# Cosine attention and a two-layer product on one core: quad 4 transposed in a visit of the first output stage, two quads' loads asked within the W1 stage, other amounts between the visits

## The chip, the cores and the metric

The kernel runs as one program on one core of a Trainium2 chip. The metric is device microseconds of one execution. The engines are named as in the profile: PE is TensorE (matmuls, transposes), PEld its weight loads, ACT is ScalarE, DVE is VectorE, POOL is GpSimd, SP is SyncE, which here only asks for DMAs. POOL asks for DMAs too, on a queue of its own.

## The reference

Inputs: q, k, v of shape (8, 12, 448, 64) in float32, tau = 0.1, w_in (768, 2048) and w_out (2048, 768). The core of it:

```python
q_n = q / (np.linalg.norm(q, axis=-1, keepdims=True) + 1e-06)
k_n = k / (np.linalg.norm(k, axis=-1, keepdims=True) + 1e-06)
scores = np.matmul(q_n, k_n.transpose(0, 1, 3, 2)) / tau
attn = softmax(scores)                      # max taken off, +1e-9 in the divisor
x = (attn @ v).transpose(0, 2, 1, 3).reshape(3584, 768)
h = x @ w_in
out = (h * np.cos(h)) @ w_out               # (3584, 768) float32
```

`softmax` stands here for the three lines of the reference that compute it.

## The kernel before

**Tiling.** Four heads of one batch entry make a quad: 8 entries x 12 heads are 24 quads, numbered 0 to 23, three to a batch entry. A quad's scores are computed in 7 blocks (j = 0 to 6) of 64 keys for all 448 queries and four heads; written (quad, block), as (3,6). A block is 4 matmuls of 64x64 (`scores`, L592) into two PSUM banks, and one Exp on ACT of 128x896 out of them into a tile E (L608). The kernel takes no maximum off, since normalised vectors bound the scores. When a quad's 7 blocks are done, `gather` (L629) multiplies the E tiles with V (28 matmuls, L637), DVE copies the result to AVs (L644), `sums` (L711) sums E over the keys and makes reciprocals, and `product` (L748, on POOL) multiplies both into xT, the input of the W1 product. R holds the reciprocals, read back from DRAM by SP's DMAs. For quad 5 the spreading is done by PE and DVE (`spread_out`).

**Before a quad's scores** come: the loads of its Q and K (`load_qk`, L442, two DMAs of 448 KB on SP's queue, into one of three buffers Qf and Kf), the squares on POOL (L491), their sums on DVE (L495), a Ln, an Exp, an add and a reciprocal for the norm (`inverse`, L521 to L530), the scaling on POOL (`scale`, L542, tiles Qn and Kn), and the transposition to qT and kT. For quads up to 5 the transposition is done by PE (`transpose`, L557): 7 matmuls of L564 for Qn, 7 for Kn, each into one PSUM bank, and two copies out of PSUM, on DVE (L575) or on ACT (L572). Later quads are transposed by DMA (`turn`, L580), asked for by SP.

**Stages.** Quads 0 to 2 are done ahead (to about 32 us). Then a loop over the batch entries c = 0 to 7 (L1093) runs two stages for each entry. The *W1 stage* computes h in 8 pairs of 128 columns (`m1_part`, L774, 12 matmuls a pair) and for each pair h*cos(h) by four operations: ACT rounds (L792), DVE reduces the argument (L793), ACT takes the Sin (L795), DVE multiplies (L798) into gT; the last pair is cut in halves. The *output stage* multiplies gT with w_out (`m2`, L833, 6 x 16 matmuls for c = 0) and, between these matmuls, does the scores of later quads. Exp and Sin need different tables on ACT; L412 loads one, 1.3 us, at each change of stage.

**Visits.** The scores of an output stage come in visits (`visits_of`, `visit`): three blocks each, after the second block of a visit the gather that is owed from the quad ended before. The first output stage (c = 0) does quads 3 to 7 in 12 visits: visit 1 is (3,0), (3,1), (3,2); visit 2 is (3,3), (3,4), (3,5); visit 3 is (3,6), (4,0), (4,1); visit 4 is (4,2), (4,3), gather of quad 3, (4,4), and the transposes of quad 5; visit 5 is (4,5), (4,6), (5,0); visit 6 (5,1), (5,2), gather of quad 4, (5,3), and so on. Ahead of visit 1 and after each visit, `fill(n)` (L1141) puts n matmuls of L833; for c = 0 the amounts are the 13 entries of `FILLS` (L860). Every block, gather and PE transposition in a visit takes the next of three slots of two PSUM banks (`slot`, L892) in turn, so the fourth after a given one must wait until that one has been read out.

**Orders.** PE does its work in the order in which the program writes it down. The order of the other engines is made by the planner (`pass_`, L121): a simulated time and for each operation a due time, worked back from PE's order. Operations are numbered as they are written down. `LEADS` (L107) adds a shift to the due times of a run of numbers: (first number, how many, shift in us), a negative one for earlier. Before the change (578, 8, -2.3) names the norm and the scaling of quad 10 and the first block (8,0) with its Exp, at the start of the second output stage; (1169, 8, -11.0) names operations of pairs 4 and 5 of a later W1 stage; (811, 8, -0.5) the table load, norm and scaling at the start of the third output stage. The orders hold through semaphores: an engine that comes to an operation whose data isn't there waits, and everything behind it on that engine with it. DMAs asked for by SP keep the order of the text for quads from 5 on, and those asked for by POOL all do.

**The places of the change.** In the W1 stage of c = 0, after pair 4, PE transposes quad 3 into the two banks of `last`; after pair 5, quad 4 into those of `av`; Q is copied out by DVE, K by ACT (L1122 to L1124). Pairs 6 and 7 then use the same banks. The loads of quads 6 and 7 stand behind the norms of quads 3 and 4 (L1087 to L1090): they may start as soon as the buffer, in which quads 3 and 4 lie, has been scaled. Quad 6 is squared early, into the tiles R (`SPARE`, L470, L1127), and its square sums are taken in visit 1 of c = 0 (L1177); quad 7 is squared in visit 3 (L906).

Of the kernel before, what the change touches and what calls it, by code (L numbers as in the profile page):

```python
# [20 lines left out]
class Planner:  # L21
# [10 lines left out]
    FIRST, LAST, CROWD = 0.6, 1.0, 1.11  # L32
# [49 lines left out]
    def flow(self, until):  # L82
# [22 lines left out]
                return o  # L105

    LEADS = (  # L107
        (1169, 8, -11.0),
        (578, 8, -2.3),
        (811, 8, -0.5),  # L110
    )

# [192 lines left out]
def bass_cosine_attention__then__act_gcu_kernel(  # L305
# [19 lines left out]
    FIRST = 3  # L325
# [51 lines left out]
    P = Planner()  # L377
# [64 lines left out]
    def load_qk(qd, after=()):  # L442
        return [load_one(qd, w, after=after) for w in range(2)]
# [413 lines left out]
                    op("sp", 0.6, lambda e, sg=sg, dst=dst: e.dma_start(dst, osb[so].ap()[64 * sg:64 * sg + 64, :]),  # L857
                       r=[("o", so, 0), ("o", so, 1)], w=[("out", t, sg)], dma=("store", so, sg), moves=0.56)

    FILLS = {0: [17, 12, 12, 6, 3, 6, 0, 13, 0, 14, 6, 3, 0]}  # L860
    STEPS = [35,28,21,21,21,21, 0, 0]
    MOST, WE = 14, (3, 2)
    ROUNDS = [[FIRST, FIRST + 1], [FIRST + 2]] + [[i, i + 1] for i in range(FIRST + 3, NQ, 2)]
# [32 lines left out]
    def visit(what):  # L896
        for qd, j in what:
            if j == 0:
                begin(qd)
            if j is None:  # L900
                gather(qd, slot())
            else:
                scores(NJ * qd + j, slot())
        for qd, j in what:
            if j == 0 and FIRST < qd < NQ - 3:
                norm_a(qd + 3, [o for o in P.ops if o.eng == "dve"][-1:])  # L906
            if j == 3 and FIRST < qd < NQ - 4:
                load_qk(qd + 4)
            if (qd, j) == (FIRST + 1, 3):
                bs = slot()  # L910
                for w in range(2):
                    transpose(FIRST + 2, w, bs + w)
            if j == NJ - 1 and qd + 2 < NQ:
                if qd > FIRST:
                    turn(qd + 2)
# [169 lines left out]
    P.arrange(HEAD)  # L1085
    ended = [o for o in P.ops if o.eng == "act"]
    norm_b(FIRST, after=ended[-1:])  # L1087
    load_qk(FIRST + 3)
    norm_b(FIRST + 1, after=ended[-1:])
    load_qk(FIRST + 4)  # L1090

    done = NJ * FIRST
    for c in range(B):  # L1093
# [20 lines left out]
        for pr in range(NNB // 2):  # L1114
            m1_part(c, pr, at_bank[pr], order if pr < early else (0, 1), late if pr < early else 0, NKC)
            if pr == 0 and c >= EC:
                if c == EC:
                    carried.extend(r for r in ROUNDS if r[-1] == done // NJ - 1)
                while carried:
                    sums(carried.pop(0), av if c > EC else last)  # L1120
            m1(c, pr, at_bank[pr])
            if c == 0 and 4 <= pr <= 5:  # L1122
                for w in range(2):
                    transpose(FIRST + pr - 4, w, (last, av)[pr - 4] + w, eng=("dve", "act")[w])  # L1124
        if c == 0:
            norm_a(FIRST + 2, [o for o in P.ops if o.eng == "dve"][-1:])
            adds = [square(SPARE, w, "pool") for w in range(2)]  # L1127
# [103 lines left out]
```

## Time and profile before

| what | us |
|---|---|
| median of 3 runs | 419.74 (418.62 to 419.95) |
| the profiled execution, its own time | 419.27 |
| its span in the trace | 417.5 |
| PE busy | 408.4 |
| ACT busy | 305.1 |
| DVE busy | 266.0 |
| POOL busy | 209.3 |

The span is what the trace covers, from the first to the last instruction of the execution; 1.8 us of the execution's time lie around it. "Busy" counts an engine's instructions from start to end; a matmul's end is modelled and overlaps the next one's start. In a timeline row stand start, duration, engine, line of the kernel, operation, tiles written and read, shape and count; in brackets the idle time ahead of it and what ended it. Rows of equal operations that follow one another are merged.

### The profile page before, as it was taken

How to read it: one execution, taken by the hardware profiler on the slowest of the kernel's cores; microseconds unless marked ns; L12 is line 12 of the kernel's file. 1: busy time of each engine (PE TensorE's matmuls, PEld its weight loads, DVE VectorE, ACT ScalarE, POOL GpSimd, SP SyncE). 2: the span in 40 equal slices, each digit the busy share in tenths (PEclk: the TensorE clock that was granted, in tenths of full speed). 3: DMA queues.
4: the chain of work that ended last, by engine and by line, in shares of the span. 5: the costliest groups of instructions: out<-in, count | busy, mean ns of one | idle time of the engine just before them, and what ended most of it. 6: DMA issues, size and time to landing. Idle time of an engine off the chain costs nothing.

```text
span 417.5 us, 8622 instructions
## 1 busy us (share of the span) xinstructions
PE 408.4 (98%) x3629; PEld 216.7 (52%) x3629; DVE 266.0 (64%) x359; ACT 305.1 (73%) x422; POOL 209.3 (50%) x145
## 2 busy tenths in 40 slices
PE   7999998999999999999999999999999999999997
PEld 7454544445554545555555555554554555555565
DVE  5887986638857549654985429845872328736931
ACT  6999899978888768897787747987797657605700
POOL 3668948996289862588419762477403113000000
PEclk9999999999999999999999999999999999999999
DMA  8999997999349994199617993099303523021023
GB/s 270 260 252 216 270 198 150 209 294 262 90 89 238 248 269 107 42 224 249 154 16 179 167 338 98 10 220 174 91 2 82 129 67 101 1 77 38 2 69 82
DMA packets 67223, 62.97 MB, mean 151 GB/s; under 512 B 36384, under 2 KB 59632, under 8 KB 67184
## 3 DMA queue, kind: packets, MB, share of 16 engines
q1 hardware_dynamic: 54816, 50.57, 47.9%
q0 software_dynamic: 12288, 11.80, 17.8%
q8 instruction: 28, 0.46, 0.4%
q14 instruction: 11, 0.09, 0.1%
q10 hardware_dynamic: 80, 0.05, 0.0%
HBM read 54.79 MB, written 11.15 MB: 158 GB/s over the span
## 4 chain that ended last, share of the span: by engine, by line
PE 80%; ACT 7%; DVE 5%; POOL 3%; DMA 2%; issue 1%; SPq 1%; POOLq 0%
PE PS L833 32%; PE PS L774 31%; PE PS L601 7%; PE PS L637 6%; ACT E L608 4%; PE PS L724 3%; DVE gT L798 2%; DVE ar L793 1%; DMA Qf<-in_q_dram 1%; DMA Kf<-in_k_dram 1%; POOL Qn L542 1%; POOL sqq L491 1%; PE PS L810 1%; ACT ar L676 1%; DVE AVs L644 1%
## 5 line engine op out<-in xcount | busy, mean ns | idle before, releaser
L608 ACT ACTIVATE E<-PS 128x896 bf16<-128x896 f32 x168 | 143.5, 921 | 20.5 <-PE PS L601 19.2
L833 PE MATMUL PS<-W,gT 128*128 128x384 bf16 x880 | 153.4, 327 | 0.0
L774 PE MATMUL PS<-xT,W 128*128 128x448 bf16 x768 | 147.7, 353 | 0.4 <-POOL xT L748 0.3
L833 PEld LDWEIGHTS PS<-W,gT 128*128 128x128 bf16 x880 | 81.9, 98 | 69.1 <-issue 16.0
L774 PEld LDWEIGHTS PS<-xT,W 128*128 128x128 bf16 x768 | 74.3, 98 | 71.3 <-issue 1.5
L792 ACT ACTIVATE ar<-PS 128x896 int32<-128x896 f32 (+1 forms) x72 | 58.8, 827 | 47.0 <-PE PS L774 46.9
L793 DVE SCALAR_TENSOR_TENSOR ar<-ar,PS 128x896 f32<-128x896 int32 (+1 forms) x72 | 69.2, 980 | 34.0 <-ACT ar L792 34.0
L748 POOL TENSOR_TENSOR xT<-AVs,R 128x896 bf16<-128x896 f32 x20 | 41.7, 2089 | 65.9 <-DMA R<-rscr 65.9
L798 DVE TENSOR_TENSOR gT<-PS,ar 128x896 bf16<-128x896 f32 (+1 forms) x72 | 69.3, 983 | 1.9 <-ACT ar L795 1.6
L795 ACT ACTIVATE ar<-ar 128x896 f32<-128x896 f32 (+1 forms) x72 | 60.6, 861 | 8.5 <-DVE ar L793 7.8
L851 DVE COPY osb<-PS 128x384 f32<-128x384 f32 x54 | 30.0, 556 | 53.6 <-PE PS L833 52.9
L542 POOL TENSOR_TENSOR Qn<-Qf,rr 128x896 bf16<-128x896 f32 x21 | 35.4, 1685 | 44.5 <-DVE rr L530 44.4
L601 PE MATMUL PS<-qT,kT 64*64 64x448 bf16 x672 | 48.9, 358 | 2.8 <-DVE kT L575 1.4
L644 DVE COPY AVs<-PS 128x896 f32<-128x896 f32 x21 | 22.8, 1088 | 35.3 <-PE PS L637 35.3
L491 POOL TENSOR_TENSOR sqq<-Qf 128x896 bf16<-128x896 f32 x21 | 35.2, 1677 | 7.3 <-DVE n L495 5.5
L491 POOL TENSOR_TENSOR sqk<-Kf 128x896 bf16<-128x896 f32 x21 | 35.2, 1676 | 6.2 <-DVE Kn L542 6.1
L542 POOL TENSOR_TENSOR Kn<-Kf,rr 128x896 bf16<-128x896 f32 (+1 forms) x22 | 36.7, 1666 | 0.0
L637 PE MATMUL PS<-E,Vb 64*64 64x448 bf16 x588 | 31.5, 350 | 0.4 <-ACT E L608 0.4
L601 PEld LDWEIGHTS PS<-qT,kT 64*64 64x64 bf16 x672 | 15.2, 105 | 27.3 <-issue 10.9
L451 POOL DMA_DIRECT2D Vb<-in_v_dram x24 | 18.1, 755 | 16.7 <-PE PS L601 10.3
L495 DVE TENSOR_REDUCE n<-sqk 128x14 f32<-128x896 bf16 (+2 forms) x24 | 24.9, 1039 | 1.8 <-POOL sqk L491 1.2
L495 DVE TENSOR_REDUCE n<-sqq 128x14 f32<-128x896 bf16 (+2 forms) x24 | 24.8, 1037 | 0.8 <-POOL sqq L491 0.6
(68 smaller groups left out, 200.5 us busy)
## 6 DMA issues: line engine op xcount, KB each, us to landing
Qf<-in_q_dram SPq DMA_DIRECT2D x24, 448.0 KB, 5.1
out_dram<-osb SPq DMA_DIRECT2D x54, 192.0 KB, 2.8
Kf<-in_k_dram SPq DMA_DIRECT2D x23, 448.0 KB, 6.1
R<-rscr SPq DMA_DIRECT2D x40, 224.0 KB, 4.4
Vb<-in_v_dram POOLq DMA_DIRECT2D x24, 224.0 KB, 5.9
W<-in_moe_w_in_dram POOLq DMA_DIRECT2D x4, 768.0 KB, 10.7
W<-in_moe_w_out_dram POOLq DMA_DIRECT2D x4, 768.0 KB, 12.5
Kf<-in_k_dram SPq DMA_DIRECT2D x1, 320.0 KB, 4.6
```

The lines of the kernel that those rows point to most:

```text
L491: op(eng, (1.64 if eng == "pool" else 1.05) * n, lambda e: e.tensor_tensor(dst, src, src, ALU.mult), r=cut(nm + "f", s, part), w=at, after ...
L495: return op("dve", 0.05 + 0.94 * n, lambda e: e.tensor_reduce(out=n2[u].ap()[:, H * w:H * w + H] if part == ALL[0] else jr(n2[u], w, part) ...
L542: lambda e: e.tensor_tensor(n[u].ap()[:, j0:j1].rearrange("p j r d -> p r j d"), f[s].ap()[:, :, j0:j1], rb, ALU.mult),
L601: ins = e.matmul(bank(bs + r, S, 64 * a, 64 * a + 64), kT[u].ap()[64 * r:64 * r + 64, j, a, :], qT[u].ap()[64 * r:64 * r + 64, :, a, :], s ...
L608: act("exp", 0.806, lambda e: e.activation(E[es].ap(), two(bs), ACT.Exp, bias=0.0, scale=INV_TAU), r=pair(bs), w=[("E", es)], chain="E")
L637: ins = e.matmul(bank(bs + a, S, 64 * r, 64 * r + 64), Vb[vs].ap()[64 * a:64 * a + 64, r, j, :], E[es[j]].ap()[64 * a:64 * a + 64, r, :], ...
L774: ins = e.matmul(bank(bk + i2), W1.ap()[:, i, 128 * nb:128 * nb + 128], xT[c % 2].ap()[:, i, :], start=(i == 0), stop=(i == NKC - 1))
L792: op("act", 0.055 + 0.375 * n, lambda e: e.activation(ai, src, ACT.Identity, bias=0.25, scale=INV2PI), r=bs, w=at)
L793: op("dve", 0.06 + 0.47 * n, lambda e: e.scalar_tensor_tensor(a, ai, -2.0 * math.pi, src, ALU.mult, ALU.add), r=bs + at, w=at)
L795: act("sin", 0.09 + 0.375 * n, lambda e: e.activation(a, a, ACT.Sin, bias=GUARD * math.pi / 2.0, scale=GUARD), r=at, w=at)
L798: op("dve", 0.07 + 0.47 * n, lambda e: e.tensor_tensor(gT.ap()[:, f0:f1, col:col + S], src, a, ALU.mult), r=bs + at, w=[("g", c % 2, f) fo ...
L833: ins = e.matmul(bank(bk, HW), gT.ap()[:, f, col:col + 128], W2.ap()[:, f, HW * h:HW * h + HW], start=(f == 0), stop=(f == NNB - 1))
```

## The change

Five edits. (1) Quad 4 is no longer transposed after pair 5 of the first W1 stage but at the end of visit 2 of the first output stage (after (3,5)), in a slot of its own, so that the visits behind it take their slots one place further on; both its copies are on DVE. (2) Quad 3 is transposed where it was, and its K copy moves from ACT to DVE. (3) The loads of quads 6 and 7 are written down after pairs 4 and 5 of the W1 stage, each behind the last operation of its pair (the DVE operation of L798). (4) `FILLS` of c = 0 has other entries; their sum stays 92. (5) Two of the three `LEADS` are others. Nothing that is computed changes.

```diff
     LEADS = (
-        (1169, 8, -11.0),
-        (578, 8, -2.3),
+        (585, 1, 3.1),
+        (560, 4, -19.9),
         (811, 8, -0.5),
     )
...
-    FILLS = {0: [17, 12, 12, 6, 3, 6, 0, 13, 0, 14, 6, 3, 0]}
+    FILLS = {0: [18, 12, 0, 9, 3, 10, 0, 15, 0, 16, 6, 3, 0]}
...
                 load_qk(qd + 4)
+            if (qd, j) == (FIRST, 5):
+                bs = slot()
+                for w in range(2):
+                    transpose(FIRST + 1, w, bs + w, eng=("dve", "dve")[w])
             if (qd, j) == (FIRST + 1, 3):
...
     norm_b(FIRST, after=ended[-1:])
-    load_qk(FIRST + 3)
     norm_b(FIRST + 1, after=ended[-1:])
-    load_qk(FIRST + 4)
...
             m1(c, pr, at_bank[pr])
-            if c == 0 and 4 <= pr <= 5:
+            if c == 0 and pr in (4,5):
+                load_qk(FIRST + 3 + (4,5).index(pr), after=P.ops[-1:])
+            if c == 0 and pr == 4:
                 for w in range(2):
-                    transpose(FIRST + pr - 4, w, (last, av)[pr - 4] + w, eng=("dve", "act")[w])
+                    transpose(FIRST, w, last + w, eng=("dve","dve")[w])
```

`FIRST` is 3.

## The prediction

> **What bounds the kernel now.** First the head of the page: span and busy time of each engine.
>
> ```profile
> span 417.5 us, 8622 instructions
> ...
> PE 408.4 (98%) x3629; PEld 216.7 (52%) x3629; DVE 266.0 (64%) x359; ACT 305.1 (73%) x422; POOL 209.3 (50%) x145
> ```
>
> TensorE (PE) is busy for all but 9.1 of 417.5 us. The change takes no matmul out and adds none, so it can only win or lose PE's waits. The next view is the busy time of each engine in stretches of the span, read for where PE does not fill its stretch.
>
> ```profile
> 44.00:52.00 8.00, 7.92 (x56) 4.47 (x54) 7.04 (x9) 6.67 (x9) 7.98 (x8) 1.00 1.20 267
> 52.00:57.00 5.00, 4.61 (x36) 2.36 (x35) 4.96 (x8) 4.68 (x7) 0.74 (x2) 1.00 1.30 203
> ...
> 62.00:67.00 5.00, 4.52 (x66) 2.36 (x64) 1.43 (x3) 4.68 (x8) 4.06 (x3) 1.00 0.55 124
> 67.00:72.00 5.00, 4.38 (x67) 1.96 (x70) 3.99 (x7) 4.54 (x7) 4.80 (x3) 1.00 0.96 156
> ...
> 82.00:90.50 8.50, 8.50 (x85) 3.67 (x83) 4.05 (x7) 7.41 (x11) 8.50 (x5) 1.00 1.08 271
> 90.50:111.00 20.50, 20.50 (x131) 10.39 (x129) 16.31 (x17) 16.11 (x21) 12.05 (x9) 1.00 0.96 231
> ...
> 148.00:417.50 269.50, 266.35 (x2149) 141.57 (x2148) 160.64 (x202) 179.60 (x235) 100.24 (x63) 1.00 0.48 114
> ```
>
> Columns: stretch, its length, then PE, weight loads, VectorE (DVE), ScalarE (ACT), GpSimd (POOL), clock, DMA share, GB/s. The clock is 1.00 throughout. The change lies between 44 and 90.5. There PE lacks 0.08 + 0.39 + 0.48 + 0.62 = 1.57 us. After 148 it lacks 3.15 us, and the chain of waits says where:
>
> ```profile
> 414.39 0.36 DVE osb L816
> ```
>
> The last PE work is over at 414.4, so 3.1 of the 3.15 us is the closing store; no wait is left there to win. Each wait of the first output stage stands in PE's timeline (start, duration, line, tiles, count, idle before and its releaser):
>
> ```profile
> 46.69 0.55 PE L564 MATMUL PS<-ident,Qn 128*128 128x128 bf16 x7
> ...
> 47.47 4.70 PE L774 MATMUL PS<-xT,W 128*128 128x448 bf16 x24
> 52.01 2.93 PE L833 MATMUL PS<-W,gT 128*128 128x384 bf16 x17
> 54.86 0.57 PE L601 MATMUL PS<-qT,kT 64*64 64x448 bf16 x8
> 55.83 0.38 PE L601 MATMUL PS<-qT,kT 64*64 64x448 bf16 x4 [0.39 <-DVE gT L798]
> ...
> 58.20 0.76 PE L601 MATMUL PS<-qT,kT 64*64 64x448 bf16 x12
> ...
> 62.72 0.82 PE L601 MATMUL PS<-qT,kT 64*64 64x448 bf16 x8
> 63.97 1.52 PE L637 MATMUL PS<-E,Vb 64*64 64x448 bf16 x28 [0.43 <-ACT E L608]
> ```
>
> ```profile
> 66.98 0.57 PE L601 MATMUL PS<-qT,kT 64*64 64x448 bf16 x8
> 68.17 0.38 PE L601 MATMUL PS<-qT,kT 64*64 64x448 bf16 x4 [0.61 <-DVE kT L575]
> ```
>
> The rows hold: the transposes of quad 4, the last W1 matmuls, the first 17 of L833, the scores of visit 1 (two blocks, then the third), of visit 2 and visit 4, the gather of quad 3, and visit 5. A matmul of L833 takes (54.86 - 52.01)/17 = 0.168 us from start to start, a block of scores 0.19 (0.76 for three, less the pipelined end), the two transposes 47.47 - 46.69 = 0.78. The printed idle understates a wait, because a row counts a matmul's pipelined end as busy. From start to start, the third block of visit 1 loses 55.83 - (54.86 + 0.38) = 0.6 us, the gather 0.7 with the block before it (63.97 against 62.72 + 0.38 + 0.19 of slower block starts), the third block of visit 5 0.8 (68.17 against 66.98 + 0.38).
>
> **Part 1: quad 4 leaves the W1 stage.** What happens at its end is set by DVE, with ACT beside it:
>
> ```profile
> 44.26 0.62 DVE L575 COPY qT<-PS 128x896 bf16<-128x896 bf16 x1
> ...
> 49.48 2.09 DVE L798 TENSOR_TENSOR gT<-PS,ar 128x896 bf16<-128x896 f32 x2 [0.56 <-ACT ar L795]
> ...
> 53.62 2.15 DVE L798 TENSOR_TENSOR gT<-PS,ar 128x896 bf16<-128x896 f32 x3
> 55.81 1.08 DVE L495 TENSOR_REDUCE n<-sqq 128x14 f32<-128x896 bf16 x1
> ```
>
> ```profile
> 45.03 0.91 ACT L572 ACTIVATE kT<-PS 128x896 bf16<-128x896 bf16 x1
> 46.89 0.92 ACT L792 ACTIVATE ar<-PS 128x896 int32<-128x896 f32 x1 [0.94 <-PE PS L774]
> ...
> 54.54 1.28 ACT L412 ACT_TABLE_LOAD   x1
> ...
> 61.38 4.16 ACT L608 ACTIVATE E<-PS 128x896 bf16<-128x896 f32 x5
> ```
>
> The row at 55.81 is the first reduction that DVE does when the stage is over. PE gives up 0.78 us of transposes. The first L833 matmul would come at 52.01 - 0.78 = 51.2. ACT gives up both copies at L572, 0.9 us each; DVE gives up one copy (qT of quad 4) and takes one (kT of quad 3), so its work stays: from 44.26 on two copies of 0.54, seven wide operations of 1.00 (the second of the pair at 49.48) and four halves of 0.55, together 10.3 us. It now ends at 53.62 + 2.15 = 55.8, so it idles 1.2 us on the way: it queues for the transposes that leave, and for a Sin behind the ACT copy. Of this I leave it 0.45 (it has finished what is ready at about 47.3, and ACT's row for the next pair, at 46.89, ends at 47.8). DVE ends at 55.0, 0.8 sooner (bounds 0 and 1.2). The table load of 1.28 and the first Exp follow the last Sin and come 0.8 sooner too, near 55.1. PE arrives at visit 1 after 18 matmuls: 51.2 + 18 x 0.168 = 54.25, and its third block waits for 55.05: 0.4 instead of 0.6. **Gain 0.2.**
>
> The Trainium skill (VectorE: DVE Perf Modes, Specifications) places ScalarE nearer PSUM and VectorE nearer SBUF, which speaks against giving a copy out of PSUM to DVE. The rows have 0.62 us on DVE (44.26) against 0.91 on ACT (45.03), so the measurement decides for DVE; were the page's placement to rule the time and the copy to cost DVE 0.91 as well, DVE would end 0.3 us later and the gain of 0.2 be gone.
>
> **Part 2: quad 4 in visit 2.** Visit 2 follows the third block of visit 1 by 58.20 - 55.83 = 2.37 us (12 matmuls as before), so it starts at 57.4. How soon Exp follows its scores: the scores of visit 3 in the chain of waits, whose Exp is the row at 61.38 above.
>
> ```profile
> 61.02 0.34 PE PS L601 x4
> ```
>
> Exp starts 0.36 after its scores, steps by (4.16 - 0.92)/4 = 0.81 and frees its banks 0.95 after its start. The transposes take the slot of block (3,3), whose Exp runs 57.8 to 58.7; PE is there at 57.4 + 0.57 = 58.0 and **waits 0.7**. They run to 59.5, and no matmuls of L833 follow (the third entry of the amounts is 0). Block (3,6) goes at once. Block (4,0) needs the slot of (3,5), free at 57.8 + 1.62 + 0.95 = 60.4, and the two DVE copies, 59.2 + 1.1 = 60.3. PE is there at 59.7: **0.7 more**. Queued behind it are (4,1) and all of PE's later work. Added: 1.4 us. ACT alone sets 1.3 of it, so that is the lower bound; if a reduction of 1.08 us (row 55.81) runs ahead of the copies it is 2.5.
>
> **Part 3: what the new amounts take off.** ACT runs ahead: Exp of (3,6) starts near 60.25 instead of 61.38. PE is behind by 11 matmuls (30 done, not 41), which it owes later as cover. After visit 3 come 9 instead of 6: PE reaches the gather of quad 3 at 60.95 + 0.1 + 1.5 + 0.4 = 62.95, and its last Exp is done at 60.25 + 1.62 + 0.95 = 62.8, so of that wait 0.6 goes. The gather ends 1 us sooner, hence the DVE copy behind it and the two copies of quad 5 (66.5 instead of 68.1), while PE reaches the block that needs them at 66.5: the wait of 0.8 becomes 0 to 0.6; I take half off, 0.4. Then there are short waits of the weight loads:
>
> ```profile
> PEld PS L601 <- ACT E L608: 1.0, 4, 0.3
> ```
>
> With ACT a microsecond ahead and 10, 15 and 16 matmuls in place of 6, 13 and 14 I take off 0.6 of the 1.0 (bounds 0 and 1.0).
>
> **Part 4: the loads of quads 6 and 7.** Four DMAs of 448 KB, on SP's queue:
>
> ```profile
> 37.23 0.37 SPq L439 DMA_DIRECT2D Qf<-in_q_dram  x1
> ...
> 42.16 0.37 SPq L439 DMA_DIRECT2D Kf<-in_k_dram  x1
> 63.68 0.37 SPq L439 DMA_DIRECT2D Qf<-in_q_dram  x1
> ```
>
> SP now asks for them from 37.23 to 42.16 and then for nothing before 63.68. Behind gT of pairs 4 and 5 (49.48 to 51.57 now, some 0.7 sooner after) they are asked at about 49.9 to 51.2. No other request stands behind them in that time, so the new wait holds nothing else on SP. Landing takes, for the first Q and the last K:
>
> ```profile
> DMA to landing us min/median/max: 7.0/7.0/7.0
> ```
>
> ```profile
> DMA to landing us min/median/max: 9.1/9.1/9.1
> ```
>
> That is 44.2 to 51.3, one in 2.35 us. Asked late, they land at about 57, 59, 61.5 and 64. GpSimd needs them:
>
> ```profile
> 47.08 1.69 POOL L491 TENSOR_TENSOR R<-Qf 128x896 bf16<-128x896 f32 x1
> ...
> 56.98 1.67 POOL L491 TENSOR_TENSOR sqq<-Qf 128x896 bf16<-128x896 f32 x1 [4.26 <-DVE n L495]
> ...
> 61.97 1.69 POOL L542 TENSOR_TENSOR Qn<-Qf,rr 128x896 bf16<-128x896 f32 x1 [1.67 <-DVE rr L530]
> ...
> 85.02 4.15 POOL L748 TENSOR_TENSOR xT<-AVs,R 128x896 bf16<-128x896 f32 x2
> ```
>
> The squares of quad 6 (47.08 and right behind it) must wait. They fall into the idle 4.26 us ahead of 56.98 and after it: about 57 to 58.7 and 59.2 to 60.9. Qn of quad 5 starts at 61.97 now and can start then. So those two are covered. The two squares of quad 7 (56.98 now) are pushed behind Kn of quad 5, near 64.3, into a stretch where GpSimd is nearly full (8.50 of 8.50 us in 82 to 90.5). Of 3.4 us pushed back, 1.0 returns by the earlier Qn and 1.1 in the idle time of 62 to 72 (4.06 and 4.80 us busy of 5.00 each); 1.3 remain. The cover is the slack between the last xT product (85.02 + 4.15 = 89.2) and the W1 matmuls that read it:
>
> ```profile
> 90.35 2.43 PE L774 MATMUL PS<-xT,W 128*128 128x448 bf16 x12
> ```
>
> That is 1.2 us, about enough: cost 0, bounds 0 and 2.2 (all 3.4 kept, less the slack). A gain is excluded, since no row above has PE waiting for a load or for GpSimd.
>
> The Trainium skill (DMA: Bandwidth & Descriptors, Rules for kernel authors) advises to issue a DMA early and wait late; this change does the opposite, and rival B is what it would cost.
>
> **Part 5: the three shifts of order.** Counted from the code, the new amounts make 22 groups of output matmuls in this stage, not 24, so every later operation's number falls by 2: (811, 8) now names what were 813 to 820. The old entry at 578 put the norms of quad 10 before the second Exp of the next stage; the new one at 585 puts that Exp back by 3.1: the same order. The entries at 560 and 1169 touch W1 stages in which PE has no idle time (20.50 of 20.50 us in 90.5 to 111). Cost 0; bounds -0.3 and +1.0 (one ACT operation of 0.92 in the way).
>
> **The sum.** -0.2 + 1.4 - 0.6 - 0.4 - 0.6 = -0.4 us against the profiled execution's 419.27 us (its span 417.5 and 1.8 around it): **418.9 us**. The median of the three runs is 419.74, so this is 0.8 below it, of which 0.5 is the difference between the executions.
>
> **The rivals.** *A: a real gain.* If Exp of visit 2 starts sooner than I put it (DVE's idle 0.45 gone as well) and the waits of visits 4 and 5 and on the weight loads go wholly, the sum is -0.4 + 1.3 - 0.6 - 0.8 - 1.0 = -1.5, **417.8 us**; with part 5's -0.3 it is 417.5. For it: ACT is the partner of every wait removed. Against it: two waits on the same ACT come in at visit 2. *B: late loads, the slower side.* If the loads land later than 61 and a square of quad 7 stands ahead of Qn of quad 5 on GpSimd, the transposes of quad 5 slip by 1.68 each, PE behind them, and the products lose their 1.2 us of slack: -0.4 + 1.7 = +1.3 for one square, +3.0 for two, **420.6 to 422.3 us**. It decides from the point where K of quad 7 lands after 61 and the order keeps it ahead. For it: the fuller GpSimd; against it: 9.1 us was the longest landing. *C: copies behind reductions.* DVE has four reductions to do between 55 and 61 (two of them of quad 6, which now come late); one ahead of the copies adds 1.1, **420.0 us**, two add 2.2, 421.1. For it: they come due at that time; against it: the copies are wanted first by PE, which the order weighs. *D: the moves change nothing*, because quad 4's transposes are hidden either way and PE's waits only shift (for it: 1.57 us in all are few; against it: DVE's end is reset by work that leaves): **419.3 us**.
>
> **Chances.** Forecast 0.34, D 0.08, A 0.30, B 0.17, C 0.11. A measurement of this kernel tells some 0.3% (1.26 us) from no change. Of A nearly all is faster by more than that; B nearly all slower; C half within, half (with two reductions) slower; a little of the forecast falls out on either side: faster 0.31, within 0.45, slower 0.24. The range leaves out the outer parts of A and B: 417.2 to 421.4; the forecast's own is 418.2 to 419.8.
>
> **What would show it.** Right: the first L833 matmul near 51.2, L572 gone, two L564 between visits 2 and 3 with about 0.7 us of idle before and after, the gather of quad 3 without idle, the Qf requests near 50, squares of R near 57. Wrong: PE idle before the transposes of quad 5 with POOL as releaser (B), a DVE reduction between the transposes of quad 4 and their copies (C), or idle time at 90 before L774.

## The result, and the profile after

| kernel | median | lowest to highest | runs |
|---|---|---|---|
| before | 419.03 us | 418.21 to 419.95 | 19 |
| after | 420.62 us | 419.36 to 423.43 | 19 |

The ratio is 1.0043 with a 95% interval of 1.003 to 1.0057: the change costs 0.4%. The time lies inside the range that was given, on the other side of the forecast. The profiled execution of after took 420.21 us, 0.94 more than that of before; the medians lie 1.59 apart. Head of its page:

```profile
span 418.4 us, 8620 instructions
...
PE 407.1 (97%) x3629; PEld 215.9 (52%) x3629; DVE 266.6 (64%) x361; ACT 304.1 (73%) x420; POOL 209.1 (50%) x145
```

Where the 0.94 us stand is read from PE's timeline: a stage begins with its first row of L774 (W1) or of L833 (output) and ends where the next begins. From the third output stage on, the lengths agree within 0.02 us in all kernels below; the head, before the first W1 stage, is 32.02 us in before and 32.08 in after.

| stage | before | after | difference |
|---|---|---|---|
| first W1 | 19.99 | 18.95 | -1.04 |
| first output | 38.34 | 40.07 | +1.73 |
| second W1 | 19.70 | 20.35 | +0.65 |
| second output | 35.21 | 35.20 | -0.01 |
| third W1 | 20.16 | 19.71 | -0.45 |
| sum of the five | 133.40 | 134.28 | +0.88 |

Busy time by stretches, columns as in the prediction (stretch, length, PE, PEld, DVE, ACT, POOL, clock, DMA share, GB/s):

```profile
57.00:62.00 5.00, 2.84 (x42) 1.40 (x39) 3.23 (x8) 4.28 (x7) 3.36 (x2) 1.00 1.17 287
62.00:67.00 5.00, 4.87 (x69) 2.88 (x66) 3.35 (x7) 4.66 (x7) 4.89 (x3) 1.00 0.92 201
67.00:72.00 5.00, 5.00 (x69) 2.21 (x70) 2.57 (x5) 4.21 (x5) 5.00 (x5) 1.00 0.81 189
...
90.50:111.00 20.50, 20.03 (x132) 9.90 (x125) 14.90 (x15) 15.32 (x19) 13.24 (x12) 1.00 1.14 273
```

In 62 to 72 PE loses 0.13 us where it lost 1.10: the waits that the amounts were to take off are gone. In 57 to 62 it loses 2.16 where it lost nothing, and in 90.5 to 111 0.47 where it lost nothing. PE's timeline names these waits:

```profile
51.03 3.09 PE L833 MATMUL PS<-W,gT 128*128 128x384 bf16 x18
...
55.05 0.38 PE L601 MATMUL PS<-qT,kT 64*64 64x448 bf16 x4 [0.43 <-DVE gT L798]
...
57.42 0.76 PE L601 MATMUL PS<-qT,kT 64*64 64x448 bf16 x12
58.83 0.56 PE L564 MATMUL PS<-ident,Qn 128*128 128x128 bf16 x7 [0.65 <-ACT E L608]
...
59.72 0.38 PE L601 MATMUL PS<-qT,kT 64*64 64x448 bf16 x4
61.61 0.57 PE L601 MATMUL PS<-qT,kT 64*64 64x448 bf16 x8 [1.51 <-DVE kT L575]
...
64.08 1.49 PE L637 MATMUL PS<-E,Vb 64*64 64x448 bf16 x28
...
102.36 9.25 PE L774 MATMUL PS<-xT,W 128*128 128x448 bf16 x48 [0.47 <-DVE gT L798]
```

The row at 61.61 is block (4,0): 1.51 us for the DVE copies of quad 4. DVE and POOL, each from its own timeline:

```profile
59.41 1.09 DVE L495 TENSOR_REDUCE n<-R 128x14 f32<-128x896 bf16 x1 [1.64 <-POOL R L491]
60.41 0.61 DVE L575 COPY qT<-PS 128x896 bf16<-128x896 bf16 x1
60.94 0.61 DVE L575 COPY kT<-PS 128x896 bf16<-128x896 bf16 x1
```

```profile
57.63 1.68 POOL L491 TENSOR_TENSOR R<-Qf 128x896 bf16<-128x896 f32 x1 [8.28 <-DMA Qf<-in_q_dram]
...
86.63 4.12 POOL L748 TENSOR_TENSOR xT<-AVs,R 128x896 bf16<-128x896 f32 x2 [0.90 <-DMA R<-rscr]
```

DVE stands 1.64 us ahead of a *reduction of quad 6* (its input R is the square that POOL wrote), and the two copies of quad 4, for which PE waits, come behind it at 60.41 and 60.94. POOL stands 8.28 us for the Q of quad 6. The chain of waits says the same in one line of descent, from SP's asking at 49.76 (start, duration, what):

```profile
49.76 7.80 DMA Qf<-in_q_dram
...
57.63 1.69 POOL R L491
...
59.41 1.09 DVE n L495
...
61.61 0.41 PE PS L601 x4
...
80.80 1.02 SPq L585
...
82.50 4.05 DMA R<-rscr
...
96.44 1.65 POOL sqk L491
...
98.11 1.09 DVE n L495
...
102.36 9.25 PE PS L774 x48
```

Two things come together at block (4,0): the load is asked late, and on DVE an operation that needs it stands ahead of one that doesn't. At the end of the stage POOL is late once more: the transposes of quad 7 (L585) wait on SP for POOL, the loads of R stand behind them, then xT, and POOL goes on from there to the square at 96.41, for which the second W1 stage's DVE waits. (x1 shows that this second part comes without a late load too.)

### The profile page after: what moved, and what is told of

It is laid out like the page before. It is cut to its first block, busy times and chain, and to the rows that moved or that the text cites. A ratio compares the mean times of both kernels' runs of the same rounds, so it can differ in the third digit from the quotient of the medians.

```text
span 418.4 us, 8620 instructions
## 1 busy us (share of the span) xinstructions
PE 407.1 (97%) x3629; PEld 215.9 (52%) x3629; DVE 266.6 (64%) x361; ACT 304.1 (73%) x420; POOL 209.1 (50%) x145
## 4 chain that ended last, share of the span: by engine, by line
PE 82%; DVE 5%; POOL 4%; DMA 4%; ACT 3%; issue 1%; SPq 1%; DVEq 0%; POOLq 0%
PE PS L833 32%; PE PS L774 32%; PE PS L601 7%; PE PS L637 6%; PE PS L724 3%; ACT E L608 2%; DMA Qf<-in_q_dram 2%; DVE n L495 1%; DMA Kf<-in_k_dram 1%; DMA R<-rscr 1%; POOL Qn L542 1%; POOL sqq L491 1%; POOL sqk L491 1%; DVE gT L798 1%; POOL xT L748 1%
## 5 line engine op out<-in xcount | busy, mean ns | idle before, releaser
L833 PE MATMUL PS<-W,gT 128*128 128x384 bf16 x880 | 153.2, 327 | 0.0
L774 PE MATMUL PS<-xT,W 128*128 128x448 bf16 x768 | 147.5, 353 | 0.5 <-DVE gT L798 0.5
L833 PEld LDWEIGHTS PS<-W,gT 128*128 128x128 bf16 x880 | 82.0, 98 | 69.0 <-issue 15.8
L774 PEld LDWEIGHTS PS<-xT,W 128*128 128x128 bf16 x768 | 74.4, 98 | 71.4 <-issue 1.5
L798 DVE TENSOR_TENSOR gT<-PS,ar 128x896 bf16<-128x896 f32 (+1 forms) x72 | 69.4, 983 | 1.4 <-ACT ar L795 1.0
```

The source lines that it names most:

```text
L774: ins = e.matmul(bank(bk + i2), W1.ap()[:, i, 128 * nb:128 * nb + 128], xT[c % 2].ap()[:, i, :], start=(i == 0), stop=(i == NKC - 1))
L798: op("dve", 0.07 + 0.47 * n, lambda e: e.tensor_tensor(gT.ap()[:, f0:f1, col:col + S], src, a, ALU.mult), r=bs + at, w=[("g", c % 2, f) fo ...
L833: ins = e.matmul(bank(bk, HW), gT.ap()[:, f, col:col + 128], W2.ap()[:, f, HW * h:HW * h + HW], start=(f == 0), stop=(f == NNB - 1))
```

## The experiments

The table gives the five stages of each kernel's profiled execution and the times of its runs; the text behind it goes through the experiments. "Early" means that the four loads don't wait for the W1 stage.

| kernel | loads | first W1 | first output | second W1 | third W1 | sum of five | median (runs) | ratio to before, 95% |
|---|---|---|---|---|---|---|---|---|
| before | early | 19.99 | 38.34 | 19.70 | 20.16 | 133.40 | | |
| after | late | 18.95 | 40.07 | 20.35 | 19.71 | 134.28 | 420.62 (19) | 1.0043 (1.003 to 1.0057) |
| x0_after_again | late | 18.96 | 39.32 | 19.87 | 19.93 | 133.28 | 422.26 (12) | 1.0052 (1.0019 to 1.0085) |
| x1_data_early | early | 18.95 | 39.73 | 20.54 | 19.70 | 134.13 | 419.61 (12) | 1.0002 (0.9971 to 1.0033) |
| x2_red_behind | late | 19.56 | 39.37 | 20.38 | 19.70 | 134.22 | 421.02 (12) | 1.0016 (0.9987 to 1.0046) |
| x3_both_behind | late | 18.95 | 40.05 | 19.70 | 19.71 | 133.61 | 420.08 (12) | 1.002 (0.9986 to 1.0054) |
| x4_before_late | late | 19.99 | 38.64 | 19.70 | 20.06 | 133.60 | 420.05 (12) | 1.0013 (0.9988 to 1.0038) |
| x5_loads_early | early | 18.95 | 44.13 | 21.04 | 19.70 | 139.03 | 424.99 (6) | 1.0141 (1.0106 to 1.0175) |
| x7_quad7_early | early | 18.95 | 39.15 | 19.70 | 19.71 | 132.71 | 418.25 (12) | 0.9976 (0.9956 to 0.9996) |
| x10_early_red | early | 19.04 | 39.65 | 19.70 | 19.70 | 133.30 | 418.89 (12) | 0.9975 (0.9948 to 1.0003) |
| x11_one_later | later | 18.95 | 40.10 | 20.44 | 19.70 | 134.40 | 422.55 (10) | 1.0066 (1.0032 to 1.01) |
| x13_two_later | later | 18.95 | 47.39 | 20.53 | 20.29 | 142.37 | 425.77 (4) | 1.0134 (1.0087 to 1.0182) |

The second output stage is 35.20 or 35.21 in all. Medians carry the head too, which varies from one execution to the next (the first W1 stage starts between 31.6 and 36.2 us in these profiles, by when W1 lands), so the stages are the finer measure of one execution and the ratios that of many. The intervals of x1 to x4 all hold 1 and all overlap that of after: by their medians none of the four can be told from before, nor from after, and what they show rests on one profile each.

### x1: the loads early, every engine's order as after

```diff
         self.order = self.pass_(shift)
+        for o in self.held:
+            o.deps = [d for d in o.deps if self.ops[d].eng != "dve"]
...
-                load_qk(FIRST + 3 + (4,5).index(pr), after=P.ops[-1:])
+                P.held += load_qk(FIRST + 3 + (4,5).index(pr), after=P.ops[-1:])
```

The orders are made with the late loads; then the loads' wait for gT is dropped.

> The changed kernel with the same order on every engine, but the four loads of quads 6 and 7 are not held behind gT of pairs 4 and 5: they start as soon as their buffers are free. Theory L (late landing: Qf of quad 6 lands 2.3 us after the place its square has in the order, the DVE reduction of that square stands ahead of the copies of quad 4, and GpSimd stays 2 us late into the next W1 stage): the idle time of PE before block (4,0) falls from 1.5 us to about 0.5, the 0.5 us before L774 at 102 goes, and the kernel is 1.5 to 2 us faster than the changed one, 0.999 to 1.000 of the kernel before. Theory S (the place of quad 4's transposes and the new amounts cost it, whatever the loads do): PE still loses 1.5 us or more at visit 3, ratio 1.003 or above. Theory O (the shifts of order in later stages): the stretch to 111 us gets better or not, but the end stays 1.003 or above.

PE's timeline (block (4,0), the end of the stage, the second W1 stage), then POOL's:

```profile
64.72 0.57 PE L604 MATMUL PS<-qT,kT 64*64 64x448 bf16 x8 [0.54 <-DVE kT L578]
...
93.92 0.50 PE L836 MATMUL PS<-W,gT 128*128 128x384 bf16 x2
94.84 2.43 PE L777 MATMUL PS<-xT,W 128*128 128x448 bf16 x12 [0.42 <-ACT E L611]
...
106.29 9.25 PE L777 MATMUL PS<-xT,W 128*128 128x448 bf16 x48 [0.67 <-DVE gT L801]
```

```profile
89.96 2.08 POOL L751 TENSOR_TENSOR xT<-AVs,R 128x896 bf16<-128x896 f32 x1 [1.08 <-DMA R<-rscr]
92.61 2.08 POOL L751 TENSOR_TENSOR xT<-AVs,R 128x896 bf16<-128x896 f32 x1 [0.57 <-DMA R<-rscr]
```

The wait ahead of (4,0) falls from 1.51 to 0.54 us, as it must if the late load made it. But the stage wins only 0.34 us, because a new wait stands at its end: the last two L833 matmuls start at 93.92 and the first of L774 at 94.84, 0.92 us later, where two matmuls take 0.34. The bracket names an Exp; the second product ends at 92.61 + 2.08 = 94.69, which fits the start of the W1 matmuls that read it. And POOL's own work does not hold the products up here: it stands idle for R ahead of each.

The other half of theory L fails. The wait in the second W1 stage does not go: it is 0.67 us (row at 106.29) where after has 0.47, and the five stages together are 0.15 us shorter than after's, not 1.5 to 2. The loads are early in x1, but the orders are those made for late loads: POOL has the squares of quad 7 behind Qn and Kn of quads 5 and 6 (35.7 us behind the start of the first W1 stage; before has them 25.0 behind it). So the late load makes the wait ahead of (4,0), and the order that was made for it is enough to keep POOL late.

### x2 and x3: the loads late, the reductions behind

```diff
+    MOVES = ((317, 334),)               # x2
+    MOVES = ((317, 334), (479, 530))    # x3
...
         self.order = self.pass_(shift)
+        for x, y in self.MOVES:
+            o = self.ops[x]
+            self.order.remove(o)
+            k = self.order.index(self.ops[y]) + 1
+            self.order.insert(k, o)
```

A move puts an operation directly behind another one of its engine. 317 is quad 6's first reduction, 334 the kT copy of quad 4; 479 is the K reduction that stands ahead of pair 1 in the second W1 stage, 530 the gT operation of that pair.

> The changed kernel with one DVE operation moved in DVE's order: the first reduction of quad 6's squares (tile R) stands behind the two copies of quad 4 instead of ahead of them. The loads stay late. Theory L: PE's idle time before (4,0) falls from 1.5 us to about 0.5, as in the run with early loads, but GpSimd stays late and the 0.5 us before L774 near 102 stays: 0.8 to 1.1 us faster than the changed kernel, ratio 1.001 to 1.002. Theory S: no change of the wait, which would then be ACT's Exp or the slot. Theory O: no change at the end.

> As the run before, and the K reduction of the quad that is normed in the second W1 stage stands behind the L798 of pair 1 there, not ahead of the L793 of pair 1. Theory L: both waits on late GpSimd work are gone from PE's path, L774 runs through without the 0.5 us, ratio 0.999 to 1.001, though every load and square is as late as in the changed kernel. Theory S and theory O: as the run before, 1.002 or above.

PE's timeline, block (4,0), first of x2, then of x3:

```profile
61.52 0.57 PE L619 MATMUL PS<-qT,kT 64*64 64x448 bf16 x8 [0.54 <-DVE kT L593]
```

```profile
62.77 0.57 PE L619 MATMUL PS<-qT,kT 64*64 64x448 bf16 x8 [0.55 <-DVE kT L593]
```

With the load as late as before, and only the order on DVE other, the wait is 0.54 as with early loads. So neither the lateness nor the order makes it alone; it takes both. x2's output stage is 0.70 us shorter than after's, but its first W1 stage is 0.61 longer, with a wait that lies ahead of the moved operation: PE comes later to block (4,0) for another reason too, and over both stages x2 gains 0.09 us. x3 has the first W1 stage of after, 18.95, and the same short wait, so there it is the order alone. x3 also shows the second half: its second W1 stage is 19.70 as in before, where x2 keeps 20.38. Its output stage is 40.05 all the same, since 0.90 us lie between the last two L833 and the first L774, as in x1: what is won at (4,0) is lost at the end, for which xT comes too late.

### x4: before, with the loads late

```diff
-    load_qk(FIRST + 3)
...
-    load_qk(FIRST + 4)
...
+            if c == 0 and pr in (4,5):
+                load_qk(FIRST + 3 + (4,5).index(pr), after=P.ops[-1:])
```

> The kernel before with one edit alone: the loads of quads 6 and 7 held behind gT of pairs 4 and 5; quad 4 is transposed in the W1 stage and the amounts are the old ones. Theory L: GpSimd comes 1.5 to 2.5 us late into the stretch from 64 on and the squares of quad 6 wait for their loads until about 57; the copies of quad 4 are long done, so PE loses nothing at visit 3, but the DVE reductions of quad 6 stand in the way of something else near 58 to 62 (copies of osb, the norm of quad 5) and the second W1 stage is touched: 0.5 to 1.5 us slower than before, ratio 1.001 to 1.004. Theory S: same as before, 0.999 to 1.001. Theory O: the same, 0.999 to 1.001.

In its profile edit 3 alone costs 0.30 us in the output stage and nothing in the second W1 stage, which theory L had expected to be touched; the sum is 0.20 over before's, less than the 0.5 to 1.5 us expected. Without quad 4's copies in visit 2, no urgent DVE work stands behind quad 6's reduction. The late loads are dear only together with edit 1.

### x5: edit 3 undone, the orders made anew

```diff
+    load_qk(FIRST + 3)
...
+    load_qk(FIRST + 4)
...
-            if c == 0 and pr in (4,5):
-                load_qk(FIRST + 3 + (4,5).index(pr), after=P.ops[-1:])
```

> Edit 3 undone: the loads of quads 6 and 7 are asked where the kernel before asks them, everything else as after, and all orders worked out anew from that. Theory L (the late landing costs twice: the copies of quad 4 wait behind the reduction of quad 6, and GpSimd enters the second W1 stage late): TensorE's wait ahead of the first block of quad 4 falls from 1.5 us to 0.6 or less. But the new order has quad 9's Qn between the two xT products and a Kn behind them, so the products end some 3 us later than in the order of after, and the second W1 stage, which reads them, stands still for about 3.5 us at its third quad: first output stage plus second W1 stage 61.5 to 63.5 us against 60.42 in after, time 421.5 to 423.5. Rival T (the two moved transposes are the cost, the loads none): the wait ahead of the first block of quad 4 stays, and the time is that of after within 0.5 us.

PE's timeline, then busy time by stretches:

```profile
60.27 0.57 PE L601 MATMUL PS<-qT,kT 64*64 64x448 bf16 x8 [0.54 <-DVE kT L575]
...
94.79 3.77 PE L774 MATMUL PS<-xT,W 128*128 128x448 bf16 x12 [4.50 <-POOL xT L748]
```

```profile
94.00:96.00 2.00, 1.21 (x4) 0.54 (x5) 0.00 (x0) 0.00 (x0) 2.00 (x2) 0.53 1.07 312
96.00:98.00 2.00, 2.00 (x8) 0.82 (x7) 0.00 (x0) 0.00 (x0) 2.00 (x3) 0.62 0.71 189
```

The wait ahead of (4,0) is 0.54, as in x1; so theory L holds for that place. The new order puts a Qn of a later quad between the two products, and PE stands 4.50 us. The products are late as a whole, too: the first starts 38.3 us behind the first output matmul, in after 35.6. Behind the wait the granted clock is 0.53 and 0.62 in two stretches of 2 us: the 12 matmuls of the row at 94.79 take 3.77 us where they take 2.43 in before, and the second W1 stage is 1.34 us longer than before's. That and a wait longer than the 3.5 us expected put the result above the 421.5 to 423.5. A plain undo would have told that the loads are better late, since it changes the orders too.

### x7 and x10: early loads, and what stands in the way of xT

x10 is x1 with the K reduction of x3 moved. x7 is x10 and besides:

```diff
+    MOVES = ((347,300),(349,347),     # POOL: squares of quad 7 behind those of quad 6
+             (348,368),(350,389),     # DVE: their reductions earlier
+             (374,392),(375,374),     # ACT: the norm of quad 7 earlier
+             (404,403),               # ACT: the Exp of Zs directly behind its Ln
+             (479,530))               # DVE: as in x3
```

> As x1_data_early (loads early, engine orders of after), and quad 7 is normalised earlier: its two squares on GpSimd directly behind those of quad 6, its two reductions on VectorE and its square root and reciprocal on ScalarE some 2 us earlier, the exponential of the sums (Zs) directly behind their logarithm, and the K reduction of quad 9 behind the gT additions of pair 1 as in x3. Theory R (the end of the output stage waits for xT, and xT for the loads of R, which stand on SyncE's queue behind the transposes of quad 7, which wait for GpSimd's Qn and Kn of quad 7): R is asked 2 us or more earlier than in x1 measured from the first output matmul (29.9 us there), the products start 1 us earlier, the 0.92 us wait between the output stage and the second W1 stage goes: output stage 38.8 to 39.0, second W1 stage 19.7; first W1 stage to the end 132.4 against 133.40 of before and 134.29 of after, so 418.0 to 418.6 where before is 419.3. Rival G (GpSimd's own queue is what makes xT late): the products start less than 0.5 us earlier, output stage 39.4 to 39.7, sum 133.0 to 133.3.

> As x1_data_early with one VectorE operation moved: the K reduction of quad 9 behind the gT additions of pair 1 in the second W1 stage. Theory L and R alike: the second W1 stage falls from 20.54 in x1 to 19.70, the output stage stays at 39.7 with its 0.92 us wait for xT; sum from the first W1 stage to the end 133.3, that is before's 133.40 within 0.2. If the late GpSimd itself (and not the reduction ordered ahead) holds the second W1 stage up, it stays over 20.2.

The chain to xT starts at Zs. In x1 its Ln is done at once and its Exp, which makes the reciprocal, comes behind three Exp of scores; ACT's and SP's timelines of x1:

```profile
76.64 0.54 ACT L736 ACTIVATE Zs<-PS 128x448 f32<-128x448 f32 x1 [0.52 <-PE PS L727]
...
79.78 0.58 ACT L737 ACTIVATE Zs<-Zs 128x448 f32<-128x448 f32 x1
```

```profile
82.42 2.56 SPq L588 DMA_TRANSPOSE kT<-Kn  x1
85.03 2.51 SPq L746 DMA_DIRECT2D R<-rscr  x4
```

SP asks for R only behind both transposes of quad 7. The same queue in x7, and POOL's products:

```profile
75.50 1.23 SPq L606 DMA_TRANSPOSE kT<-Kn  x1
76.78 3.90 SPq L764 DMA_DIRECT2D R<-rscr  x4
```

```profile
83.78 4.12 POOL L769 TENSOR_TENSOR xT<-AVs,R 128x896 bf16<-128x896 f32 x2
```

Measured from the first output matmul (55.11 in x1, 50.58 in x7), R is asked at 26.2 instead of 29.9, and the products start at 33.2 instead of 34.9, without idle time. The 0.92 us at the stage's end is gone: the stage is 39.15 against 39.73, a little over the 38.8 to 39.0 expected. This is as theory R has it; rival G, by which the products would come less than 0.5 us earlier, falls. Eight operations are moved at once, and which of them does it was not run apart.

x10 shows the second W1 stage alone: 19.70 with products about as late as in x1 (34.7 us behind the first output matmul). Its output stage, 39.65, is the 39.7 that was expected, but by luck: a wait of its own, 0.91 us for a part of w_out, comes early in the stage, and PE is then so late that at its end next to nothing of the wait for xT is left (0.39 us for two matmuls of 0.34).

What the second W1 stage costs shows over several kernels. The K reduction, ahead of pair 1 or behind it on DVE, reads a square of POOL's; its start is counted from the start of the stage.

| kernel | K reduction | start of the square | second W1 |
|---|---|---|---|
| before | ahead | 3.71 | 19.70 |
| x0 | ahead | 4.83 | 19.87 |
| after | ahead | 5.31 | 20.35 |
| x1 | ahead | 5.50 | 20.54 |
| x3 | behind | 5.49 | 19.70 |
| x10 | behind | 5.50 | 19.70 |

From 4.83 on the stage grows by as much as the square is later. So here too it takes both, as at block (4,0): before has the reduction in the same place and pays nothing, since its POOL is early.

x7 is a little faster than before, 0.9976 with an interval of 0.9956 to 0.9996, and took 418.25 us where after, on the same chip, took 422.26.

### x0: after once more

> The changed kernel unaltered, beside the three on the same chip: stages as in its first profile (18.95, 40.07, 20.35, 35.20, 19.71), 134.29 from the first W1 stage to the end, and a median 0.5 to 1.5 us over that of before. If the head, before the first W1 stage, is what made it slower, the sum differs from before's 133.40 by less than 0.3.

The profiled execution, PE's and then DVE's timeline:

```profile
60.53 0.57 PE L601 MATMUL PS<-qT,kT 64*64 64x448 bf16 x8 [0.77 <-DVE kT L575]
```

```profile
58.33 1.09 DVE L495 TENSOR_REDUCE n<-R 128x14 f32<-128x896 bf16 x1 [0.90 <-POOL R L491]
```

It is the fastest of the 12 runs, 418.86 us. The same load, asked at the same place (17.68 us behind the start of the W1 stage in both), came 0.74 us sooner: POOL's square starts 24.81 us behind that start, in after's first profile 25.55. DVE's wait is 0.90 instead of 1.64, PE's 0.77 instead of 1.51, the output stage 39.32 instead of 40.07. The same program with another landing shows what a later landing costs: as much of the stage. The sum, 133.28, is within 0.3 of before's, which by the expectation would speak for the head; but the median of the 12 runs is 422.26, 2.60 us above before's where 0.5 to 1.5 were expected, so this is the good end of after's executions and not its rule, and it can't say what makes the others slow.

### x11 and x13: the loads later still

```diff
+        gt = {w: o for o in self.ops if o.eng == "dve" and o.start < 60 for w in o.writes if w[0] == "g"}
+        for k, o in enumerate(self.held):
+            o.deps = sorted({*o.deps, gt["g", 0, 10 + 2 * (k // 2)].i})    # x13: 12
```

> After with the order on every engine kept; the loads of quad 6 wait for the gT additions of pair 5 instead of pair 4 (1.1 us later in the trace of after), those of quad 7 for pair 6 instead of pair 5. Theory L (the time of asking sets the landing): the square of quad 6 starts about 1.1 us later (58.7 where the first W1 stage starts at 32.1), VectorE waits 2.7 us ahead of the reduction instead of 1.64, TensorE 2.6 us ahead of the first block of quad 4 instead of 1.51, output stage 41.2, second W1 stage 20.4 to 21.1. Rival Q (what GpSimd's own queue still has in transfer sets the landing, not the asking): landing and waits as in after within 0.3 us.

> The same, two pairs later: quad 6 waits for the gT additions of pair 6 (4.2 us after those of pair 4), quad 7 for those of pair 7. Theory L: waits 4 us longer than in after, if the landing takes 7.8 us again, or 1.5 to 2.5 us longer, if the landing is shorter because GpSimd's queue is empty by then (4.5 to 5 us, as of the later pairs of quads); TensorE's wait ahead of the first block of quad 4 is 3 to 5.5 us, output stage 41.6 to 44. A wait of that length should also lower the granted clock behind it, as the wait of 4.50 us for xT did in x5 (0.53 and 0.62 in the next two stretches of 2 us), which costs some 1.5 us more; a wait that stays under 2 us leaves it at 1.00. Rival Q: as in after.

x11, PE's timeline; then x13's, and its busy time by stretches:

```profile
61.14 0.57 PE L615 MATMUL PS<-qT,kT 64*64 64x448 bf16 x8 [1.54 <-DVE kT L589]
```

```profile
64.61 0.96 PE L615 MATMUL PS<-qT,kT 64*64 64x448 bf16 x8 [5.03 <-DVE kT L589]
...
97.91 0.35 PE L788 MATMUL PS<-xT,W 128*128 128x448 bf16 x1 [1.24 <-ACT E L622]
```

```profile
64.00:66.00 2.00, 1.39 (x10) 0.47 (x11) 1.05 (x5) 0.74 (x1) 1.76 (x2) 0.50 0.32 98
66.00:68.00 2.00, 2.00 (x8) 0.91 (x6) 1.88 (x4) 1.44 (x4) 2.00 (x2) 0.50 0.03 13
68.00:70.00 2.00, 2.00 (x22) 0.83 (x24) 0.17 (x1) 0.86 (x2) 2.00 (x2) 0.55 0.63 147
```

In x11's profile the load, asked 1.1 us later than in after, landed no later (POOL's square starts 25.58 us behind the start of the W1 stage), and the wait is 1.54: this execution is as rival Q has it, not as theory L, though the spread of 0.74 between after and x0 leaves one profile little weight. x13 speaks for theory L. In x13, asked 4.2 us later, the square starts 29.07 us behind, 3.5 later, the wait is 5.03 us, and the granted clock falls to 0.50 for some 6 us. The output stage is 47.39, more than the 44 expected: block (4,0) comes 3.5 us later in it than in after, the work from there to the scores behind the gather of quad 3 takes 6.24 instead of 3.80 us at the lower clock, 2.4 more, and at its end PE stands for xT (1.24 us idle at 97.91, 1.4 more than in after from start to start).

The medians say more than x11's one profile: 422.55 us, 0.66% over before. Of its 10 runs 7 have a mean granted clock of 0.996 or less; of x13's all 4, of after's 9 of 31 (both sets), of x2, x3 and x4, with loads as late, 6 of 36, of before's 7 of 77, and of x1, x7 and x10 together 1 of 36; of x5's, whose loads are early and whose wait for xT is long, all 6. So with later loads the clock falls in more executions, and x5 speaks for long waits of PE, not the load as such, as what brings it. It is not all that makes after slow: of its runs beside x7, the 8 with a higher mean clock have a median of 420.77, before's 28 have 419.59. No profile of after itself with such a clock was taken, and the one fall seen in an x3 profile lies in the head (12 to 16 us). That after's slowest runs have theirs behind block (4,0) was not shown.

## Why the prediction was wrong

**Part 1 was right.** The first L833 matmul is at 51.03 (51.2 forecast), the third block of visit 1 at 55.05 (55.05). Its wait did not shrink, though: from start to start it is 0.62 us, as before, where 0.4 was forecast, since PE comes 0.2 us sooner than forecast to a block whose start DVE sets. The copies on DVE take 0.61 us (rows at 60.41 and 60.94), against the 0.91 of the ACT copy that they replace; the Trainium skill's placement of ScalarE nearer PSUM (VectorE: DVE Perf Modes, Specifications) does not show in them, and no loss came of that edit.

**Part 2 was right up to its last wait, and there failed.** Visit 2 starts at 57.42 (57.4), the transposes at 58.83 behind 0.65 us of idle time (0.7), block (3,6) at 59.72 (59.5). Block (4,0) was to start at 60.4 and starts at 61.61: 1.2 us are missing. The failing step is "the two DVE copies, 59.2 + 1.1 = 60.3", which took DVE to be free. It was standing for quad 6's square: both waits of this part together are 2.5 us from start to start (0.84 and 1.70), not 1.4, which is the upper bound that the part itself gave for a reduction ahead of the copies. Rival C named the order ("one ahead of the copies adds 1.1") and rival B the late load; I weighed them as alternatives with 0.11 and 0.17. They are one case: the load's lateness is what makes the order cost anything, as x1 and x3 show by taking one away each. My own working put the squares of quad 6 at "about 57 to 58.7", so DVE's reduction could not end before 59.8. The order could have been looked at with that number in hand; "the copies are wanted first by PE, which the order weighs" is no reason where the order is made with a landing that doesn't come: in the planner's simulated time the reduction ends 0.73 us before the copies start (57.53 and 58.26), so its place cost nothing there.

**Part 3 was right in its first two terms.** The gather of quad 3 has no idle row in after, the transposes of quad 5 none, the third block of visit 5 none: in 62 to 72 PE loses 0.13 instead of 1.10 us, where I took off 1.0 in the first two terms. PE's late coming is not the reason: in x7, which stands only 0.55 us at (4,0), the same waits are gone, and only 0.17 us ahead of the transposes of quad 5 are new. The weight loads' 0.6 can't be told from these rows.

**Part 4 failed.** "Cost 0" rested on slack of 1.2 us between the last product and the W1 matmuls. The products start 1.6 us later (86.63 for 85.02), so the slack is gone, but the first W1 matmul of the second stage lost little to it (0.34 us, no more than two matmuls, lie between the last L833 and the first L774), because PE itself comes 0.75 us later there. Where that is mended, in x1 and x3, the same place costs 0.56 us (0.90 to 0.92 less 0.34). So in after two delays of nearly one length run side by side, and to take away one of them wins little: that is why x1's output stage gains 0.34 us and x3's nothing. The price fell further on: POOL's squares of the next quads come 2.35 us later (96.41 for 94.06), DVE meets one of their reductions ahead of the gT operations, and PE stands 0.47 us at 102.36; +0.65 in the stage. I had followed the late operation to the next reader and not to the one behind it. That the slack was used up also has a second reason that I did not see: R is asked for behind quad 7's transposes, so POOL's lateness reaches xT through SP. The Trainium skill's advice to issue a DMA early and wait late (DMA: Bandwidth & Descriptors, Rules for kernel authors) holds here, with a proviso from x4: in its profile late loads alone cost 0.2 us; they are dear where urgent work is queued behind their reader.

**Part 5 and the rest.** I wrote that no wait was left behind 148 and looked at nothing between 111 and 148; before has one there, PE standing for xT (0.29 us idle, PE's timeline of before):

```profile
147.22 0.93 PE L774 MATMUL PS<-xT,W 128*128 128x448 bf16 x4 [0.29 <-POOL xT L748]
```

It is gone in after, and the third W1 stage is 0.45 us shorter. POOL's product starts 0.16 us ahead of the stage's first matmul in before and 0.68 ahead in after, where PE comes later; but in x7 it starts 1.03 ahead, though PE comes no later than in before (113.0 and 113.2 us behind the start of the first W1 stage), so PE's lateness is not the only reason, and which edit brings the rest was not shown. This gain was not foreseen. The new amounts and the two new shifts of LEADS were not run apart from the rest.

**The sum.** Forecast -0.4. Add 1.2 for block (4,0), 0.65 for the second W1 stage, take off 0.45 for the third: +1.0, and +0.94 was measured between the two profiled executions; the 1.59 of the medians is not explained to the end. x7, where both losses are mended, has a sum of -0.69 against before. Of this -0.45 is the third W1 stage, which the forecast doesn't have; the first two, of which the forecast speaks, have -0.23 against its -0.4. To that extent its terms were sound, though not for early loads alone: x1 is still 0.73 over before. (Rival A's sum holds a +1.3 for which the text gives no source.)

## What to carry to other kernels

A load that is asked later costs not where it is read but where urgent work is queued behind its reader on an in-order engine: follow each late value through the queue of every engine that touches it, the second queue too, before its cost is put at nothing. An order that was made for late loads keeps part of its cost when the loads come early (x1). Where a change moves loads and computation together, test with the orders held fixed; an undo that lets the orders be made anew (x5) measures another kernel. And one profile of a kernel whose loads land just in time is one draw: the same program gave 418.86 and 424.76 us.

## What the runs showed of the hardware

The granted clock fell to a half while PE stood for 4.50 us (x5) and for 5.03 us (x13); it stayed at 1.00 through waits of 1.51 (after), 1.54 (x11) and 2.48 us (x1, ahead of its first W1 stage, for W1). In short stretches the trace shows where in the wait it falls, first x13, then x5 (columns as above, the clock third from the end):

```profile
62.80:63.00 0.20, 0.00 (x0) 0.00 (x0) 0.20 (x1) 0.00 (x0) 0.00 (x0) 0.95 1.11 371
63.00:63.20 0.20, 0.00 (x0) 0.00 (x0) 0.20 (x1) 0.00 (x0) 0.00 (x0) 0.50 1.08 378
```

```profile
94.00:94.20 0.20, 0.00 (x0) 0.00 (x0) 0.00 (x0) 0.00 (x0) 0.20 (x1) 0.78 1.10 440
```

PE's last matmuls ahead of the waits end at 59.59 and 90.29, so the fall comes 3.4 us into the one wait and 3.8 us into the other. The clock is back at about 97.5 in x5, 3.4 us after it fell, and at about 69.8 in x13, 6.8 us after. So a long wait is paid for a second time in part: 1.3 us behind the 4.50, 2.4 behind the 5.03, each read from the rows that the lower clock lengthens. The Trainium skill (TensorE: Matmul & The Clock Gate, Part 1: The HAM clock gate) gives half the clock after an idle window of about 3.4 us; the two falls agree with it.

A load of 448 KB asked while POOL's own loads of V and w_out were running came 6.8 to 8.2 us behind its asking in the seven executions with late loads (from SP's row to POOL's first square: 49.76 to 57.63 in after, 49.42 to 56.55 in x0, 50.64 to 57.63 in x2, 51.89 to 60.05 in x3, 50.81 to 57.95 in x4, 50.36 to 57.16 in x11, 53.46 to 60.64 in x13). Between after and x0, which are one program, 0.74 us of the place of a wait is left to chance.
